# Four more first-weight loads inside the recurrence loop, and four reorderings in the last part of an mLSTM + soft-MoE kernel

## The chip, the cores and the metric

The kernel runs on one core of a Trainium2 chip. The metric is the device time of one execution in microseconds; three executions of the kernel before gave 192.66, 192.68 and 195.63 us, with a median of 192.68. One more execution was taken with the hardware profiler, and its trace is the source of all durations below.

## What is computed

Two parts follow each other. The first is a recurrent cell over 768 steps for 4 x 8 heads of width 40; its output is scaled by a sigmoid gate and becomes a matrix x of 3072 tokens x 320 features. The second is a soft mixture of experts: every token gets 32 logits, the 32 slots are weighted sums of all tokens, 8 experts each turn 4 slots through two layers, and every token takes a weighted sum of the slots' outputs.

```
for t in range(S):
    m_new = maximum(f[t] + m, i[t])
    C = exp(f[t] + m - m_new) * C + exp(i[t] - m_new) * outer(v[t], k[t])
    n = exp(f[t] + m - m_new) * n + exp(i[t] - m_new) * k[t]
    y[t] = sigmoid(o[t]) * (C @ q[t]) / maximum(abs(n . q[t]), 1)
x = y as (B * S, H * D)                 # 3072 x 320
logits = x @ phi                        # 3072 x 32
d = softmax of logits over the tokens   # per slot
slot_in = d.T @ x                       # 8 experts x 4 slots x 320
h = maximum(slot_in[e] @ w1[e], 0)      # w1: 8 x 320 x 1024
slot_out[e] = h @ w2[e]                 # w2: 8 x 1024 x 320
c = softmax of logits over the slots    # per token
out = c @ slot_out
```

## The kernel before, in words

The recurrence is computed in chunks. 24 steps (`NSTEP`) each handle 64 time steps of two of the four batches, so a step yields 128 tokens. Its products within the chunk are `scores` (queries times keys, into `psc`), the decay weights `ew` come from an exponential (`expo`), `mix_s` on VectorE (DVE) multiplies scores and weights, `mix_q` on GpSimd (POOL) multiplies the queries with their weights, in two instructions for the two batches, `keys` on VectorE scales the keys (`kr`), `state` carries the state on and `pv` forms the output in PSUM (`php`, later `phe` and `pzpsc`). `post_a_ops` and `post_b` divide and gate it into x, and `xtr` transposes x for the logits.

The order of all work is written out by hand; every engine runs its own instructions in program order. The main loop runs i from 0 to 20: iteration i loads KV for step i + 2, first weights (`load_w1`, 512 KB each) where i is in the list `W1L`, second weights (`load_wave`, 640 KB each, called waves) where `WVN` says so, the output gates of a group of four steps (`load_sig`, when i is a multiple of 4), and queries and keys for step i + 4; then it computes parts of steps i - 1 to i + 2. All these loads are issued by SyncE (SP) on one hardware queue, in program order. A load into a buffer that is still read makes SP wait, and all loads behind it.

Four steps are a group for the mixture of experts. For each group the loop forms the logits (`moe_pl`), the running maximum and the exponentials (`moe_nm_ops`, `ex_dT`), copies the logits (`ex_lt`, tile `lt`), transposes both and adds to the slots' running sum `acc` (`moe_psl`, `moe_acc`); `moe_e0`, `moe_e`, `comb_s` make the tokens' combine weights E, in two parts of reduced precision, and `comb_T`/`comb_h` transpose them and copy them to `cT`.

The last part begins after the loop. There step 21 is finished, steps 22 and 23 are done, and SP issues what is left of the 20 first weights and of the 16 waves; the waves reuse the buffers of the recurrence. Groups 4 and 5 (`gl - 1` and `gl`) are handled by hand: logits `pl4`, the product `psl4` in the same PSUM buffer, the final rescaling `a`, the slot inputs `psa` and `psb`, copied to `slT` by VectorE. `asum` is the slots' sum of exponentials, `pden` (one matmul with the selector `cden`) brings it to the slots' order, and `rd` is its reciprocal. `up` multiplies with the first weights in two halves of 512 columns (`phh`, `pzhm`), `relu` scales and clips, `turn` transposes, `down` multiplies with the waves, first for output columns 0 to 191 (`hf` = 0, `pso0`), then for 192 to 319. `gather` copies the result, `combine` forms the output blocks, and SP stores them. In the output loop over `PLAN` pieces of `down(1, ...)` stand between the output blocks.

Of the kernel before, what the change touches and what calls it, by code (L numbers as in the profile page):

```python
# [7 lines left out]
F32 = mybir.dt.float32  # L8
F32R = mybir.dt.float32r
# [9 lines left out]
DM = H * D  # L19
# [39 lines left out]
WV1 = 5  # L59
W1L = (2, 3, 5, 6, 7, 9, 10, 11, 14, 16, 18, 19, 20)  # L60

# [7 lines left out]
def kernel(ctx: ExitStack, tc: tile.TileContext, qk, kv, og, g0, g1, g2, consts, cinit, w1, w2, out):  # L69
# [230 lines left out]

    def mix_q(i):
        if i < 2 or i >= NSTEP:
            return
        t, w = KQ[i % NQ], ew[i]
        for a, r in enumerate(rows):
            nc.gpsimd.tensor_tensor(w[r, a], t[r, 1], w[r, a], ALU.mult)  # L306

# [119 lines left out]
    def ex_lt(gi, pl):  # L427
        run["lt"] = sb.tile([P, P], F32, tag="lt", name=f"lt{gi}")
        nc.scalar.copy(run["lt"], pl)
# [44 lines left out]

    def comb_T(tag=None, bufs=1, pc=None):
        e = run["E"]
        if pc is None:
            pc = pp.tile([P, GRP, P], F32, tag=tag, name="pc", bufs=bufs)
        for j in range(GRP):
            o = pc[:, 2 * (j % 2):2 * (j % 2) + 2, 64 * (j // 2):64 * (j // 2) + 64]  # L480
            nc.tensor.transpose(o.bitcast(F32R), e[:, 4 * j:4 * j + 4].rearrange("p g w x -> p (g w x)"), identr)
        return pc
# [17 lines left out]

    def comb_hi(e):
        E = run["E"] = sb.tile([P, GRP * NS // 8, 4, 8], F32R, tag="e", name="E")
        nc.scalar.copy(E[:, :, 0:2], bcast(e))

# [3 lines left out]

    def comb_s(gi, e):
        emit(comb_s_ops(gi, e))  # L510
        comb_n(e)
        comb_hi(e)
        comb_lo(e)
# [119 lines left out]
    post_b(i - 1)  # L633
    mix_q(NL)
    mix_s(NL)
    pv(i)
    scores(NL + 1)
# [41 lines left out]
    ex_dT(gl - 1)  # L679
    al4 = run["al"]  # L680
    moe_dT(gl - 1)
    pq = pp.tile([P, 2, 512], F32, tag="pe", name="pq")
# [11 lines left out]
    pd2 = [pq[:, 1, n * P:(n + 1) * P] for n in range(2)]  # L694
    ex_lt(gl - 1, pl4)
    moe_dT(gl, d=d5)
    load_wave()

    cden = d5_[:, 3 * P:]
    for t in slT + hT + [cden]:  # L700
        nc.gpsimd.memset(t, 0.0)
# [34 lines left out]
    for n, w in enumerate((128, 128, 64)):  # L736
        o = psa if n == 0 else psb[0:w, n - 1, :]
        nc.tensor.matmul(o, acc[:, n * P:n * P + w], selw, start=True, stop=True)
    pav = psa.rearrange("p (j r q) -> p j r q", j=4, r=2)
    pbv = psb.rearrange("p c (j r q) -> p c j r q", j=4, r=2)  # L740
# [8 lines left out]

    asum = sb.tile([P, 1], F32, tag="den", name="asum", bufs=ND)  # L750
    nc.vector.tensor_tensor(asum, a, acc[:, DM:DM + 1], ALU.mult)
    phh = [pp.tile([P, 512], F32, tag="ph", name="phh0"), pz[1]]
# [24 lines left out]
    CO = (0, HC0)  # L777
    pso = [pp.tile([P, HC[0]], F32, tag="pst", name="pso0"), pp.tile([P, 2, 512], F32, tag="pe", name="pso1")[:, 0, 0:HC[1]]]

# [47 lines left out]
    up(0, range(1, 2))  # L827
    pden = pp.tile([P, 1], F32, tag="pm", name="pden", bufs=2)
    nc.tensor.matmul(pden, cden, asum, start=True, stop=True)
    rd = sb.tile([P, 1], F32, tag="rl", name="rd", bufs=3)  # L830
# [4 lines left out]
    up(0, range(3, 5))  # L835
    comb_h(gl - 1, comb_T(pc=pz[0].rearrange("p (j t) -> p j t", j=GRP)))
    moe_e(gl, e0)
    h0 = relu(0)
    comb_s(gl, run["e"])
    up(1, range(1))  # L840
# [12 lines left out]
    for q, n in enumerate(PLAN):  # L853
        for h, x in rest[:n]:
            down(1, h, [x])
        rest = rest[n:]
        if q == 0:
            comb_h(gl, comb_T(pc=pz[0].rearrange("p (j t) -> p j t", j=GRP)))
        combine(0, QO[q])
    for h, x in rest:  # L860
# [79 lines left out]
```

## Time and profile before

| | |
|---|---|
| median of three executions | 192.68 us |
| the profiled execution's own time | 191.7 us |
| its span in the trace | 189.9 us |
| PE (TensorE) busy | 153.7 us, 81% of the span |
| DVE busy | 137.1 us, 72% |
| ACT (ScalarE) busy | 104.2 us, 55% |
| POOL busy | 105.3 us, 55% |
| DMA | 46.11 MB, mean 243 GB/s, 82.9% of 16 engines on the data queue |

In rows of the trace, times are in microseconds from the start of the span. PE is the matmul, PEld the weight load that overlaps it. "out<-in" are the program's names for tiles, x8 is a count, and the bracket at a row's end tells how long the engine was idle before it and what released it; "issue" there means that the profile shows nothing that it waited for. L785 is line 785 of the kernel before. Busy shares average over stages with different limits: the loop lasts until about 134 us, the last part until the end.

### The profile page before, as it was taken

To read this page: it belongs to the slowest core of one execution; us is meant where nothing else is said; L and a number is where in the kernel's file an instruction comes from. 1 tells how busy PE (TensorE), PEld (TensorE's weight loads), DVE (VectorE), ACT (ScalarE), POOL (GpSimd) and SP (SyncE) were. 2 spreads that over 40 slices of the span, in tenths; PEclk is the share of its full clock that TensorE was granted. 3 is DMA by queue.
4 is the path that set the end of the run, shared out by engine and by line. 5 is a ranking of instruction groups with operands and counts; after the bars stand their busy time and mean duration, and the time that the engine had idled before them with its cause. 6 is when DMAs were issued, how large, how long until landed. Compare 5 with 4: busy or idle time off the path is not lost.

```text
span 189.9 us, 7226 instructions
## 1 busy us (share of the span) xinstructions
PE 153.7 (81%) x3017; PEld 118.5 (62%) x3017; DVE 137.1 (72%) x302; ACT 104.2 (55%) x233; POOL 105.3 (55%) x120
## 2 busy tenths in 40 slices
PE   7639869886899777995979968799879899949940
PEld 2328757775688755884857857588767433618740
DVE  6896999799689957599987984689866465304440
ACT  5885507856288674684848757586824512004340
POOL 8970519995688993575865789347991511000000
PEclk9975979998799997899999999999999999999996
DMA  5999693749949499273997999959999999972996
GB/s 142 238 264 249 195 303 80 236 93 309 278 105 268 118 318 272 70 254 66 279 278 199 277 298 262 257 146 274 258 385 398 364 364 363 363 253 65 298 277 198
DMA packets 25424, 46.11 MB, mean 243 GB/s; under 512 B 2224, under 2 KB 16944, under 8 KB 25392
## 3 DMA queue, kind: packets, MB, share of 16 engines
q1 hardware_dynamic: 25392, 45.65, 82.9%
q8 instruction: 24, 0.39, 0.9%
q14 instruction: 8, 0.07, 0.1%
HBM read 41.71 MB, written 3.93 MB: 240 GB/s over the span
## 4 chain that ended last, share of the span: by engine, by line
PE 44%; DVE 17%; DMA 11%; issue 10%; POOL 6%; ACT 6%; SPq 2%; DVEq 0%; POOLq 0%; ACTq 0%
DMA w<-in_w_dram 8%; PE psc L299 7%; PE php L342 5%; POOL ew L306 4%; PE pst L332 4%; DVE ew L312 4%; PE pe L282 3%; PE php L343 3%; PE pt L380 3%; PE po L814 3%; PE pso L785 2%; PE phh L757 2%; PE pl L389 2%; DVE RR L259 2%; PE pst L331 2%
## 5 line engine op out<-in xcount | busy, mean ns | idle before, releaser
L306 POOL TENSOR_TENSOR ew<-KQ,ew 40x512 f32<-40x512 f32 (+1 forms) x44 | 63.7, 1447 | 3.4
L299 PE MATMUL psc<-KQ 40*64 40x64 f32 (+1 forms) x768 | 29.6, 228 | 7.9 <-issue 4.5
L365 POOL TENSOR_TENSOR x<-sig,den 128x320 f32<-128x320 f32 x21 | 15.7, 750 | 36.2 <-DVE den L357 32.1
L312 DVE TENSOR_TENSOR ew<-psc,ew 64x512 f32<-64x512 f32 x48 | 32.2, 671 | 1.6 <-PE psc L299 0.7
L299 PEld LDWEIGHTS psc<-KQ 40*64 40x64 f32 (+1 forms) x768 | 26.1, 141 | 10.4 <-issue 4.9
L342 PE MATMUL php<-KV,ew 104*64 104x41 f32 x352 | 26.0, 236 | 3.7 <-DVE rsum L491 1.9
L343 PE MATMUL php<-KV,ew 128*64 128x41 f32 x352 | 26.3, 237 | 2.4 <-issue 1.8
L342 PEld LDWEIGHTS php<-KV,ew 104*64 104x64 f32 x352 | 23.7, 144 | 6.3 <-issue 5.3
L316 DVE TENSOR_TENSOR kr<-KV,rl 128x640 f32<-128x640 f32 x22 | 26.9, 1221 | 0.6
L284 ACT ACTIVATE ew<-pe 128x1024 f32<-128x1024 f32 x24 | 24.5, 1020 | 4.3 <-PE pe L282 4.1
L332 PE MATMUL pst<-KV,kr 128*64 128x41 f32 x352 | 26.5, 238 | 0.0
L343 PEld LDWEIGHTS php<-KV,ew 128*64 128x64 f32 x352 | 23.6, 142 | 2.6 <-issue 1.9
L384 ACT COPY xT<-pt 128x384 f32<-128x384 f32 x23 | 10.9, 479 | 24.4 <-PE pt L380 24.3
L332 PEld LDWEIGHTS pst<-KV,kr 128*64 128x64 f32 x352 | 23.7, 145 | 0.2 <-issue 0.2
L331 PEld LDWEIGHTS pst<-KV,kr 104*40 104x40 f32 x352 | 18.0, 122 | 8.8 <-issue 5.3
L282 PE MATMUL pe<-RR,LL 128*128 128x512 f32 x48 | 18.5, 468 | 3.9 <-DVE LL L268 2.5
L331 PE MATMUL pst<-KV,kr 104*40 104x41 f32 x352 | 20.8, 215 | 0.0
L334 ACT COPY KV<-pst 40x328 f32<-40x328 f32 (+1 forms) x44 | 18.8, 426 | 1.8 <-PE pst L332 0.8
L259 DVE TENSOR_TENSOR RR<-Y,hmp 32x512 fp32r<-32x512 f32 x24 | 16.3, 679 | 0.9
L380 PE MATMUL pt<-cst,x 128*128 128x128 f32 x63 | 12.1, 303 | 0.9 <-POOL x L365 0.8
L266 ACT ACTIVATE LL<-Y,cst 32x64 fp32r<-32x64 f32 x38 | 11.1, 337 | 1.8 <-DVE Y L232 1.4
L282 PEld LDWEIGHTS pe<-RR,LL 128*128 128x128 f32 x48 | 7.9, 207 | 4.6 <-ACT KV L195 2.6
(199 smaller groups left out, 244.8 us busy)
## 6 DMA issues: line engine op xcount, KB each, us to landing
w<-in_w_dram SPq DMA_DIRECT2D x20, 512.0 KB, 7.2
w<-in_w_dram SPq DMA_DIRECT2D x15, 640.0 KB, 10.4
KV<-in_kv_dram SPq DMA_DIRECT2D x48, 162.0 KB, 5.6
KQ<-in_qk_dram SPq DMA_DIRECT2D x24, 320.0 KB, 6.3
sig<-in_og_dram SPq DMA_DIRECT2D x6, 640.0 KB, 5.3
out_dram<-ob SPq DMA_DIRECT2D x5, 384.0 KB, 3.3
out_dram<-ob SPq DMA_DIRECT2D x2, 512.0 KB, 5.0
w<-in_w_dram SPq DMA_DIRECT2D x2, 320.0 KB, 9.5
```

The lines of the kernel that those rows point to most:

```text
L259: a = lambda: nc.vector.tensor_tensor(RR[n][g0:g0 + 32], y[g0:g0 + 32].unsqueeze(1).broadcast_to([32, H, L]), hmp[g0:g0 + 32, 0:H].unsquee ...
L282: nc.tensor.matmul(pe[:, a], LL[:, n, a, :], RR[n], start=True, stop=True)
L284: nc.scalar.activation(ew[i], pe, AF.Exp)
L299: nc.tensor.matmul(psc[64 * a:64 * a + 64, h], t[r, 0, h], t[r, 1, h], start=True, stop=True)
L306: nc.gpsimd.tensor_tensor(w[r, a], t[r, 1], w[r, a], ALU.mult)
L312: nc.vector.tensor_tensor(w[r, a], psc[r], w[r, a], ALU.mult)
L316: e.tensor_tensor(kr[i % 2][:, :, :, R0:], KV[i % NK][:, :, 0:DM].rearrange("p a (h d) -> p a h d", h=H), rl[i].unsqueeze(3).broadcast_to( ...
L331: nc.tensor.matmul(pst[64:64 + D, h], k[0:104, 0, h, R0:], vc[0:104, 0, h], start=True, stop=True)
L332: nc.tensor.matmul(pst[0:64, h], k[:, 1, h], vc[:, 1, h], start=True, stop=True)
L334: nc.scalar.copy(nvc[r, a], pst[r])
L342: nc.tensor.matmul(ph[0:64, h, 0:V1], w[0:104, 0, h], vc[0:104, 0, h], start=True, stop=True)
L343: nc.tensor.matmul(ph[64:128, h, 0:V1], w[:, 1, h], vc[:, 1, h], start=True, stop=True)
```

## The change

- `W1L` gains iterations 4, 8, 12 and 17: 17 of the 20 first weights are loaded in the loop, 3 behind it. At 4, 8 and 12 the added load stands between the KV loads and `load_sig`, at 17 between the KV loads and a wave.
- Of step 22's two `mix_q` instructions the second goes from POOL to VectorE, behind `mix_s` of that step.
- `ex_lt(gl - 1)`, ScalarE's copy of group 4's logits, is emitted before `moe_dT(gl - 1)` and no longer after group 5's exponentials.
- `asum` is formed on ScalarE (a copy with a per-partition scale), and the matmul `pden` goes ahead of the up-projection, into a free part of the buffer `pq`. The selector's memset goes ahead of the other memsets; its copy stays behind them.
- Group 4's `comb_T`/`comb_h` move from the middle of the up-projection into the output loop, ahead of its second block. For this group 5's E gets a buffer of its own (tag RR1) and the transposes a free PSUM bank.

```diff
-W1L = (2, 3, 5, 6, 7, 9, 10, 11, 14, 16, 18, 19, 20)
+W1L = (2, 3, 4, 5, 6, 7, 8, 9, 10, 11, 12, 14, 16, 17, 18, 19, 20)
...
-    def mix_q(i):
+    def mix_q(i, batches=(0, 1), e=nc.gpsimd):
...
-        for a, r in enumerate(rows):
-            nc.gpsimd.tensor_tensor(w[r, a], t[r, 1], w[r, a], ALU.mult)
+        for a in batches:
+            r = rows[a]
+            e.tensor_tensor(w[r, a], t[r, 1], w[r, a], ALU.mult)
...
-    mix_q(NL)
+    mix_q(NL, (0,))
     mix_s(NL)
+    mix_q(NL, (1,), nc.vector)
     pv(i)
...
     al4 = run["al"]
+    ex_lt(gl - 1, pl4)
     moe_dT(gl - 1)
...
-    ex_lt(gl - 1, pl4)
     moe_dT(gl, d=d5)
     load_wave()
...
-    for t in slT + hT + [cden]:
+    for t in [cden] + slT + hT:
         nc.gpsimd.memset(t, 0.0)
...
         nc.tensor.matmul(o, acc[:, n * P:n * P + w], selw, start=True, stop=True)
+    asum = sb.tile([P, 1], F32, tag="den", name="asum", bufs=ND)
+    nc.scalar.activation(asum, acc[:, DM:DM + 1], AF.Copy, scale=a)
+    pden = pq[:, 1, 2 * P:2 * P + 1]
+    nc.tensor.matmul(pden, cden, asum, start=True, stop=True)
...
-    asum = sb.tile([P, 1], F32, tag="den", name="asum", bufs=ND)
-    nc.vector.tensor_tensor(asum, a, acc[:, DM:DM + 1], ALU.mult)
...
-    pden = pp.tile([P, 1], F32, tag="pm", name="pden", bufs=2)
-    nc.tensor.matmul(pden, cden, asum, start=True, stop=True)
...
-    comb_h(gl - 1, comb_T(pc=pz[0].rearrange("p (j t) -> p j t", j=GRP)))
+    E4 = run["E"]
     moe_e(gl, e0)
     h0 = relu(0)
-    comb_s(gl, run["e"])
+    comb_s(gl, run["e"], "RR1")
...
             comb_h(gl, comb_T(pc=pz[0].rearrange("p (j t) -> p j t", j=GRP)))
+        if q == 1:
+            comb_h(gl - 1, comb_T(pc=pso_[:, 1].rearrange("p (j t) -> p j t", j=GRP), e=E4))
         combine(0, QO[q])
```

More of the change, by code (lines that the diff above doesn't have):

```diff
@@ L472, in moe_comb2, with comb_T @@
         comb_h(gi, comb_T("pm", 2))
-    def comb_T(tag=None, bufs=1, pc=None):
-        e = run["E"]
+    def comb_T(tag=None, bufs=1, pc=None, e=None):
+        e = e or run["E"]
         if pc is None:
@@ L499, in comb_n, with comb_hi @@
         v.tensor_tensor(e, e, run["rsum"].unsqueeze(2).broadcast_to([P, GRP, NS]), ALU.mult)
-    def comb_hi(e):
-        E = run["E"] = sb.tile([P, GRP * NS // 8, 4, 8], F32R, tag="e", name="E")
+    def comb_hi(e, tag="e"):
+        E = run["E"] = sb.tile([P, GRP * NS // 8, 4, 8], F32R, tag=tag, name="E")
         nc.scalar.copy(E[:, :, 0:2], bcast(e))
@@ L507, in comb_lo, with comb_s @@
         v.tensor_tensor(E[:, :, 2:4], bcast(e), E[:, :, 0:2], ALU.subtract)
-    def comb_s(gi, e):
+    def comb_s(gi, e, tag="e"):
         emit(comb_s_ops(gi, e))
         comb_n(e)
-        comb_hi(e)
+        comb_hi(e, tag)
         comb_lo(e)
@@ L777 @@
     CO = (0, HC0)
-    pso = [pp.tile([P, HC[0]], F32, tag="pst", name="pso0"), pp.tile([P, 2, 512], F32, tag="pe", name="pso1")[:, 0, 0:HC[1]]]
+    pso = [pp.tile([P, HC[0]], F32, tag="pst", name="pso0")]
+    pso_ = pp.tile([P, 2, 512], F32, tag="pe", name="pso1")
+    pso.append(pso_[:, 0, 0:HC[1]])
     def down(hf, n, rk):
```

## The prediction

> **What bounds the kernel now.** I read the page first (its span below), then the chain that ended last, and then the part of the PE timeline to which that chain points.
>
> ```profile
> span 189.9 us, 7226 instructions
> ```
>
> ```profile
> 160.66 10.37 DMA w<-in_w_dram
> ```
>
> This piece of the chain is the last second-weight load (a wave). It is issued at 160.66, and the matmuls that use it start when it has landed, at 171.07. The PE timeline shows how long PE stood still for it and its forerunners:
>
> ```profile
> 163.97 2.16 PE L785 MATMUL pso<-w,hTa 128*32 128x192 f32 x48
> 165.94 0.83 PE L785 MATMUL pso<-w,hT 128*32 128x192 f32 x16
> 166.59 0.51 PE L785 MATMUL pso<-w,hTa 128*32 128x192 f32 x8
> 167.62 0.53 PE L785 MATMUL pso<-w,hTa 128*32 128x192 f32 x8 [0.52 <-DMA w<-in_w_dram]
> 169.50 0.53 PE L785 MATMUL pso<-w,hT 128*32 128x192 f32 x8 [1.34 <-DMA w<-in_w_dram]
> 171.07 0.53 PE L785 MATMUL pso<-w,hT 128*32 128x192 f32 x8 [1.03 <-DMA w<-in_w_dram]
> 171.42 0.84 PE L785 MATMUL pso<-w,hTa 128*32 128x128 f32 x24
> ```
>
> Unhindered, 48 matmuls go from 163.97 to 165.94, 0.041 us each. The 96 of the first output half that follow 163.97 would be through at 163.97 + 96 x 0.041 = 167.9; the next half starts at 171.42. **The stall is 3.5 us**: three idle times, and three times the refilling of PE. Why the loads are late is seen in the DMA view from 134 to 172 us (slices of 0.95 us) and in a table by stage (PE, PEld, DVE, ACT, POOL busy, PE clock, DMA share, GB/s):
>
> ```profile
> GB/s 254 286 230 334 345 410 375 397 418 414 414 418 387 345 368 358 364 362 362 364 363 373 358 365 362 365 362 364 362 360 362 365 369 354 369 358 302 152 35 0
> ...
> w<-in_w_dram SPq DMA_DIRECT2D x7, 512.0 KB, 7.6
> ```
>
> ```profile
> 38.50:41.20 2.70, 2.10 (x55) 1.84 (x52) 2.62 (x6) 2.33 (x6) 2.55 (x4) 1.00 0.29 68
> 61.70:64.00 2.30, 1.90 (x58) 1.69 (x53) 2.22 (x9) 1.16 (x4) 2.02 (x4) 1.00 0.31 84
> 86.20:88.80 2.60, 1.11 (x34) 1.04 (x32) 2.50 (x9) 0.51 (x2) 0.81 (x1) 1.00 0.14 31
> 113.60:124.20 10.60, 8.99 (x193) 7.00 (x193) 5.59 (x12) 7.12 (x18) 6.88 (x7) 1.00 1.06 265
> 124.20:127.60 3.40, 3.40 (x88) 2.92 (x85) 3.40 (x9) 2.96 (x7) 1.05 (x1) 1.00 0.43 105
> 174.80:188.40 13.60, 7.84 (x120) 6.63 (x118) 5.43 (x12) 4.49 (x11) 0.00 (x0) 0.92 0.97 290
> ```
>
> From 134 us to the last landing the DMA engines never rest: seven first weights go first, at some 410 GB/s, then the waves at some 364. The end part is bound by bytes, while the loop leaves holes (shares of 0.29, 0.31 and 0.14).
>
> **The change part by part.**
>
> *Four first weights more in the loop.* The end part loses 4 x 524,288 bytes, at 410 GB/s 5.1 us, and every wave lands that much earlier, the last near 166.0. What is late next is PE itself: with the other edits (-0.9 together ahead of this point, below) it comes to the last wave's matmuls at 171.07 - 3.5 - 0.9 = 166.7. So the whole stall goes, **-3.5**, with 0.7 us of cover; each us by which the end part's loads start later than that comes back one for one. Bounds: -3.0 with half a us lost so, -3.7 if a matmul is 0.039.
>
> *What they cost the loop.* Iterations 4, 8 and 12 issue the added load behind the KV loads and ahead of the sig load, for which SP waits anyway:
>
> ```profile
> SPq L140 <- POOL x L365: 14.1, 4, 4.4
> ```
>
> Four waits, 14.1 us together, up to 4.4: there lie the three holes, 2.70, 2.30 and 2.60 us long. One load at the loop's 265 GB/s takes 2.0 us and fits into each, and the sig and KQ issues behind it wait for nothing new. Iteration 17 has no hole (1.06 from 113.60 to 124.20), so 2.0 us of backlog pass on, to the KQ and wave issues behind it and the next KV loads; the stretch that follows, at 0.43, has 1.9 us idle and takes them up. The new tiles reuse buffers of the gates, all done before the new iteration. What a full DMA does hold up in the loop is PE's own instructions:
>
> ```profile
> 111.73:117.64 5.91, 5.42 (x125) 4.75 (x125) 3.74 (x8) 3.97 (x10) 5.68 (x5) 1.00 1.04 292
> 117.64:141.73 24.09, 21.22 (x503) 17.88 (x503) 19.05 (x41) 14.95 (x33) 16.62 (x15) 1.00 0.93 261
> ```
>
> ```profile
> 111.73 0.25 PE L343 MATMUL php<-KV,ew 128*64 128x41 f32 x1 [1.78 <-issue]
> ```
>
> ```profile
> 117.65 0.45 PE L299 MATMUL psc<-KQ 64*64 64x64 f32 x8 [0.49 <-issue]
> ```
>
> ```profile
> 141.73 0.20 PE L343 MATMUL phe<-KV,ew 128*64 128x41 f32 x1 [0.80 <-issue]
> ```
>
> ```profile
> q8 instruction: 24, 0.39, 0.9%
> ```
>
> Before these three rows PE stands with nothing to wait for. Between the first two lie 125 + 125 matmuls and weight loads, between the last two 503 + 503, four times as many; the 24 instruction packets (0.39 MB) serve them in blocks of about that size. I read it as PE coming to the end of a block before the next one is there, where the DMA share is 0.93 or more. Behind iteration 17 a block comes due at about 129, in a stretch that the backlog now fills. I take a little under the small stall of 0.49, **+0.3**; bounds 0 and 2.0 (a stall like the largest, 1.78, and something at iteration 8).
>
> [...]
>
> *One scaling of queries on VectorE.*
>
> ```profile
> 137.20 5.42 POOL L306 TENSOR_TENSOR ew<-KQ,ew 40x512 f32<-40x512 f32 x4
> 142.59 0.72 POOL L507 TENSOR_TENSOR E<-e,E 128x256 fp32r<-128x256 f32 x1
> ```
>
> ```profile
> 142.94 0.72 DVE L365 TENSOR_TENSOR xy<-sig,den 128x320 f32<-128x320 f32 x1
> ```
>
> ```profile
> L306 POOL TENSOR_TENSOR ew<-KQ,ew x44: 1256/1272/1942, 21.7 to 141.2; 40x512 f32<-40x512 f32 x22, 64x512 f32<-64x512 f32 x22
> ```
>
> ```profile
> L316 DVE TENSOR_TENSOR kr<-KV,rl x22: 817/1214/1639, 10.9 to 134.0; 128x640 f32<-128x640 f32 x22
> ```
>
> POOL loses one of four (5.42 / 4 = 1.36 us). The piece on VectorE is bounded by kr, 640 columns and both operands in the same memory: 0.82 at the least, 1.64 at the most; POOL's own stretch from 1.26 to 1.94. So I let the new piece queue behind POOL's first and end near 139.1, and hold POOL's next back by half a us. Behind it on VectorE stand the denominators, the sig product and the scores' scaling of the last steps, which PE waits for. POOL is done near 141.6 instead of 142.6, but PE doesn't go on before 141.73, when its instructions arrive, so the 1.36 isn't gained in full. What is gained is that L507 on POOL is over before the row of 142.94 starts: while the two overlap that row takes 0.72, and I let it fall by half. **-0.35**, bounds -1.3 (PE follows POOL) and +0.5 (the slip passes on).
>
> *Logits copied sooner.*
>
> ```profile
> 147.63 0.27 PE L689 MATMUL prow<-cst,nm 128*1 128x128 f32 x1
> 148.33 0.75 PE L442 MATMUL psl<-x,d 128*32 128x321 f32 x8 [0.44 <-ACT lt L429]
> ```
>
> ```profile
> 148.03 0.25 ACT L429 COPY lt<-pl 128x128 f32<-128x128 f32 x1
> ```
>
> psl is written where the logits stood and waits for this copy. Moved ahead of the copy of the transposed weights on ACT it is done long before; psl then starts behind prow, near 147.85: **-0.5**, bounds -0.44 (the idle time) and -0.6.
>
> *Slot sums on ScalarE, their product ahead.*
>
> ```profile
> 151.58 1.92 PE L757 MATMUL phh<-w,slTx 128*32 128x512 f32 x16
> 153.44 0.38 PE L829 MATMUL pden<-asum,d 128*128 128x1 f32 x2
> ```
>
> ```profile
> 151.63 0.20 POOL L701 MEMSET d<- 128x128 f32 x1
> 151.90 0.21 POOL L702 COPY d<-cst 128x32 f32<-128x32 f32 x1
> ```
>
> The product costs PE the same as before, only ahead of the up-projection. But it needs the selector that POOL copies at 151.90, behind all its memsets. The selector's own memset, 0.20, goes to an idle time, so the copy ends near 151.9 (on the old clock), while PE is free at 151.58: PE waits 0.3 to 0.4, and the whole up-projection stands behind it. **+0.4**, bounds 0 and +0.7 (product and wait). The sum itself, on ACT, is shorter than the 0.25 of the logits' copy or near it; behind it stand only a combine copy and an exponential that nothing on PE needs then.
>
> *The fourth group's combine transposes moved into the output loop.* Four transposes leave the stretch ahead of the wait and return before the second output block, with their copy on ACT. Once the stall is gone both places count alike for PE. The stores behind them fill 0.97 of the DMA's time (174.80:188.40), so the end follows the first store. **0**; bounds -0.5 (the stores close their gaps) and +0.6 (the first store late by the extra copy).
>
> *One more instruction block* comes due on PE near 168 while waves have just landed: **+0.1**, bounds 0 and 0.5.
>
> **Sum:** -3.5 + 0.3 - 0.35 - 0.5 + 0.4 + 0 + 0.1 = -3.55. (Ahead of the last wave: -0.5 - 0.35 + 0.4 and the moved transposes, -0.5, make the -0.9 above.) The profiled execution took 191.7 us, 1.8 beside its span: 191.7 - 3.55 = 188.15. The median shown, 192.68, lies 0.98 above it, and on that I forecast **189.1**.
>
> **The rivals.**
>
> *PE follows POOL.* The idle 0.80 before 141.73 falls away because other loads are in flight, the end part starts that much sooner, and the loop costs nothing: 189.1 - 0.8 - 0.3 = 188.0. For it: the idle times differ (1.78, 0.49, 0.80). Against: the DMA is as full there as before.
>
> *New waits in the new bound.* PE is now the bound, and what hits it counts in full: the selector wait at 0.7, the ACT copy at 0.6, the slip on VectorE at half its bound: 189.1 + 0.3 + 0.6 + 0.6 = 190.6. For it: each lies on PE's way. Against: each has some cover.
>
> *The change doesn't do what it says: SP, not bytes, paces the waves.*
>
> ```profile
> 134.51 4.12 SPq L147 DMA_DIRECT2D w<-in_w_dram x7
> ```
>
> Then four issues less bring the waves forward by 4 x 4.12 / 7 = 2.4 alone, PE's early 0.9 is lost in the wait that is left, and the moved transposes cost their 0.5 behind it: 192.68 - 2.4 + 0.5 + 0.3 = 191.1. Against: the GB/s stand flat at 364, as of a full DMA.
>
> *Instruction blocks late throughout the loop (slower).* Each added load pushes one block past its need, at the price of the row at 111.73, 1.78. Two of them, 3.6, are less than the gain without the loop's term (3.85); from the third on the kernel is slower: 192.68 - 3.85 + 3 x 1.78 = 194.2. For it: the stalls seen lie where the DMA is full. Against: a hole is filled with one load, not overfilled.
>
> **How the numbers follow.** Forecast 0.50, PE follows POOL 0.22, new waits 0.16, SP paces 0.07, late blocks 0.05. The range takes in 188.0 and part of the good bounds beyond it (-0.7 more), and on the poor side 191.1 with a large loop stall in part (+1.1): 187.3 to 192.2. A measurement of this kernel can tell about 2%, which is 188.8 on the good side. Beyond it lie most of the first rival (0.20) and four tenths of the forecast (0.20): faster 0.40. Over 196.5 it comes only with a fourth late block and more: 0.02. Within: 0.58.
>
> **What would show it.** Right: no DMA idle before pso in the first half and the last wave landing near 166; psl behind prow without a wait for lt; a PE gap before pden that POOL ends; the first store some 3.5 us earlier. Wrong: "w<-in_w_dram" still ahead of pso; more "issue" idle on PE between 36 and 130 us; the last KV loads issued later than before; a first store less than 3 us earlier.

## The result, and the profile after

The changed kernel takes **190.88 us** (median of 20 executions, 188.97 to 196.75) beside 194.13 us for the kernel before (20 executions, 191.16 to 202.92). The ratio is **0.9895, 95% interval 0.9861 to 0.9928**: about 1% faster, where the forecast was 3.55 us, 1.8% of the median shown. Single executions spread over 8 us (changed) and 12 us (before), with longer times at a lower granted clock (188.97 us at 0.954, 196.75 at 0.895), and the ratio is formed from the undisturbed ones alone. By the means of these 20 and 20 the gain is 3.54 us; in a later round, with 6 executions of the changed kernel and 23 of the kernel before, it is nil (194.06 and 194.03). Over all the executions measured in rounds the mean is 194.30 us for the kernel before (89 executions, standard error 0.27) and 192.05 us for the changed one (26, 0.51), 2.25 us less. So there is a gain, but its size is known to about a us only. That 190.88 lies inside the forecast's range says little, since in this measurement the kernel before gave 194.13 and not 192.68.

The profiled execution took 190.58 us, span 188.5. The first thing to read is where the loop ends, which is the last K/V issue on SP (the first row of its pair), and where the first store goes out. Before, then after (start, length, queue, line):

```profile
133.35 0.47 SPq L133 DMA_DIRECT2D KV<-in_kv_dram  x1
...
173.83 11.42 SPq L819 DMA_DIRECT2D out_dram<-ob  x11
```

```profile
136.04 0.47 SPq L133 DMA_DIRECT2D KV<-in_kv_dram  x1
...
172.25 11.74 SPq L825 DMA_DIRECT2D out_dram<-ob  x11
```

The loop ends 2.69 us later, the first store leaves only 1.58 us earlier. Counted from that K/V issue to the end of the span, the last part went from 56.57 to 52.45 us: -4.12, where the sum (without the loop's +0.3) had -3.85. So the last part did what was forecast, and the loop gave most of it back in these two executions. The last part first, on PE. The first output half of the kernel before starts here, and its waits are shown in the prediction:

```profile
161.97 1.48 PE L785 MATMUL pso<-w,hTa 128*32 128x192 f32 x32
```

The changed kernel:

```profile
163.22 1.48 PE L791 MATMUL pso<-w,hTa 128*32 128x192 f32 x32
...
165.22 2.16 PE L791 MATMUL pso<-w,hTa 128*32 128x192 f32 x48
167.19 0.83 PE L791 MATMUL pso<-w,hT 128*32 128x192 f32 x16
167.84 0.83 PE L791 MATMUL pso<-w,hTa 128*32 128x192 f32 x16
168.49 0.95 PE L791 MATMUL pso<-w,hT 128*32 128x192 f32 x16
169.26 0.84 PE L791 MATMUL pso<-w,hTa 128*32 128x128 f32 x24
```

No row of the first output half (128x192) waits for a wave any more, where before three did. From its first matmul to the first of the second half (128x128) it is 169.26 - 163.22 = 6.04 us, before 171.42 - 161.97, some 9.44. The last wave lands at 168.87, while its matmuls are already due: the cover of 0.7 us is not there. The holes in the loop are filled, as the windows show for the same stretches as before (DMA share and GB/s last):

```profile
38.50:41.20 2.70, 2.10 (x58) 1.85 (x53) 2.62 (x6) 2.39 (x6) 2.55 (x4) 1.00 0.76 237
61.70:64.00 2.30, 1.83 (x52) 1.62 (x52) 2.20 (x9) 1.15 (x5) 2.02 (x4) 1.00 0.99 210
86.20:88.80 2.60, 1.13 (x32) 1.04 (x32) 2.49 (x10) 0.82 (x2) 1.12 (x2) 1.00 0.64 153
113.60:124.20 10.60, 7.38 (x139) 5.82 (x141) 5.04 (x10) 5.06 (x15) 5.54 (x6) 0.76 1.06 271
```

The fourth row tells what went wrong: 139 matmuls where there were 193, at a granted clock of 0.76 instead of 1.00. The K/V issues of the iterations up to 18 come within 1.4 us of where they did; that of iteration 19 comes at 124.85 before and 127.54 after. PE's own row and the clock by slices (before, then after) show what lies there:

```profile
117.98 1.14 PE L299 MATMUL psc<-KQ 64*64 64x64 f32 x30 [2.16 <-issue]
```

```profile
PEclk9975979998799997899999999999999999999996
```

```profile
PEclk9995887999699999999999999669999999999995
```

A late instruction block held PE for 2.16 us, and from 119.11 to 125.94 its clock was halved (0.50 there; the two sixes in slices 26 and 27). Before, the same block was 0.49 us late, and 3.41 us of halved clock (0.50) lay at 73.62.

That such waits are late blocks is the author's reading, in the prediction from three rows; the trace's instruction packets agree with it. The packet ahead of this wait lies at 114.95 to 116.30, and PE goes on 1.68 us later. In the fifteen profiled executions 75 waits of PE after 27 us are marked "issue" and longer than 0.4 us, and every one ends 1.2 to 1.7 us after the end of an instruction packet. One more "issue" wait per execution, of 2.1 to 3.0 us at 25.5 to 26.2 us, is of another kind: no packet ends at that distance ahead of it, and it ends 0.1 us after VectorE's last product that reads the tile `psc`, which PE writes next.

### The profile page after: what moved, and what is told of

It is laid out like the page before. It is cut to its first block, busy times and chain, and to the rows that moved or that the text cites. A ratio compares the mean times of both kernels' runs of the same rounds, so it can differ in the third digit from the quotient of the medians.

```text
span 188.5 us, 7226 instructions
## 1 busy us (share of the span) xinstructions
PE 154.7 (82%) x3017; PEld 119.6 (63%) x3017; DVE 138.5 (73%) x302; ACT 104.7 (56%) x234; POOL 104.7 (56%) x119
## 4 chain that ended last, share of the span: by engine, by line
PE 58%; DVE 18%; issue 10%; POOL 5%; DMA 3%; ACT 3%; SPq 1%; DVEq 0%; ACTq 0%; POOLq 0%
PE psc L299 9%; PE php L343 5%; PE pso L791 5%; PE pst L333 5%; PE pe L282 4%; PE pt L381 4%; DVE ew L313 3%; PE php L344 3%; PE pl L390 3%; PE pw L156 3%; DVE kr L317 3%; DMA w<-in_w_dram 3%; PE po L820 2%; PE phh L761 2%; PE pzhm L761 2%
## 5 line engine op out<-in xcount | busy, mean ns | idle before, releaser
L307 POOL TENSOR_TENSOR ew<-KQ,ew 40x512 f32<-40x512 f32 (+1 forms) x43 | 62.9, 1463 | 3.2
L366 POOL TENSOR_TENSOR x<-sig,den 128x320 f32<-128x320 f32 x21 | 15.7, 750 | 38.3 <-DVE den L358 31.7
L299 PEld LDWEIGHTS psc<-KQ 40*64 40x64 f32 (+1 forms) x768 | 25.8, 140 | 11.8 <-issue 6.0
L343 PE MATMUL php<-KV,ew 104*64 104x41 f32 x352 | 25.6, 234 | 4.6 <-DVE rsum L492 1.8
L333 PE MATMUL pst<-KV,kr 128*64 128x41 f32 x352 | 27.4, 242 | 1.1 <-issue 1.1
L317 DVE TENSOR_TENSOR kr<-KV,rl 128x640 f32<-128x640 f32 x22 | 26.4, 1202 | 0.6
L344 PE MATMUL php<-KV,ew 128*64 128x41 f32 x352 | 26.2, 236 | 0.6 <-POOL ew L307 0.6
L333 PEld LDWEIGHTS pst<-KV,kr 128*64 128x64 f32 x352 | 24.6, 149 | 1.3 <-issue 1.3
L332 PEld LDWEIGHTS pst<-KV,kr 104*40 104x40 f32 x352 | 18.5, 124 | 8.9 <-issue 6.0
L332 PE MATMUL pst<-KV,kr 104*40 104x41 f32 x352 | 21.3, 217 | 0.0
L357 DVE SCALAR_TENSOR_TENSOR sig<-sig,php 128x320 f32<-128x320 f32 x22 | 10.5, 477 | 0.2
```

What stands on the lines that cost most here:

```text
L299: nc.tensor.matmul(psc[64 * a:64 * a + 64, h], t[r, 0, h], t[r, 1, h], start=True, stop=True)
L307: e.tensor_tensor(w[r, a], t[r, 1], w[r, a], ALU.mult)
L317: e.tensor_tensor(kr[i % 2][:, :, :, R0:], KV[i % NK][:, :, 0:DM].rearrange("p a (h d) -> p a h d", h=H), rl[i].unsqueeze(3).broadcast_to( ...
L332: nc.tensor.matmul(pst[64:64 + D, h], k[0:104, 0, h, R0:], vc[0:104, 0, h], start=True, stop=True)
L333: nc.tensor.matmul(pst[0:64, h], k[:, 1, h], vc[:, 1, h], start=True, stop=True)
L343: nc.tensor.matmul(ph[0:64, h, 0:V1], w[0:104, 0, h], vc[0:104, 0, h], start=True, stop=True)
```

## The experiments

Two questions were open. The first: does the loop's loss come from the added load of iteration 17 (theory A), from the four loads together through a fuller DMA and later instruction blocks, or from something that differs between executions whatever the loads are? The second: what is the freed stall in the last part worth? The expectations name their theories by letters and say what each stands for. "Halved" is time at half clock in the loop: the stretches that begin after 18 us and before the loop's end.

**Without the load of iteration 17 (no17).**

```diff
-W1L = (2, 3, 4, 5, 6, 7, 8, 9, 10, 11, 12, 14, 16, 17, 18, 19, 20)
+W1L = (2, 3, 4, 5, 6, 7, 8, 9, 10, 11, 12, 14, 16, 18, 19, 20)
```

> The changed kernel with 16 instead of 17 first weights in the loop, iteration 17's taken back into the last part. Theory A (iteration 17's load fills a stretch in which the DMA has no room, an instruction block reaches PE late, PE stands idle for about 2 us and its clock is halved for 6.8 us): the loop ends as early as before the change (last KV issue near 133.4 us, no idle of 2 us on PE about 118), the last part gives back about 1.2 us of the stall since every wave lands 1.3 us later; together 0.5 to 1 us faster than the changed kernel, ratio to the kernel before 0.984 to 0.987. Theory B (the halved clock falls on single executions by chance, and no load in the loop costs anything): only the 1.2 us are given back, ratio 0.995 to 0.997.

Measured: median 190.59 us (187.57 to 193.5), ratio 0.988 [0.969, 1.0069], too wide an interval to tell the theories apart. Its loop ended at 137.15, not earlier but 1.1 us later than with the load; PE again stood 1.34 us before the same matmul, and half clock came at 128.34. The wave stall grew, as one more load in the last part must make it:

```profile
169.84 0.53 PE L791 MATMUL pso<-w,hT 128*32 128x192 f32 x8 [0.60 <-DMA w<-in_w_dram]
171.42 0.53 PE L791 MATMUL pso<-w,hT 128*32 128x192 f32 x8 [1.04 <-DMA w<-in_w_dram]
171.77 0.84 PE L791 MATMUL pso<-w,hTa 128*32 128x128 f32 x24
```

**The same load two iterations later (late19).** One line: 17 leaves W1L and 19 issues two.

```diff
-            if i in W1L:
+            for _ in range(W1L.count(i)):
                 load_w1(len(w1_sb))
```

> The changed kernel with iteration 17's load moved to iteration 19, which then has two. Theory A: the stretch from 113 to 124 us is as before the change and the backlog falls into one with room; the loop loses 0.3 at most and the last part keeps all its gain, ratio 0.979 to 0.983. Theory B: the same as the changed kernel, 0.988 to 0.991.

Measured: median 192.11 us (190.53 to 196.93), ratio 1.0052 [0.9973, 1.0131], which neither theory had; by the means of all executions of these rounds it is 192.89 beside 193.97. In its profile the loop ended at 140.29 with 27.3 us of halved clock; from the K/V issue of iteration 17 to that of 19 it is 17.90 us without a load at 17, in no17 15.74, in the changed kernel 16.41. PE stood 2.51 us for a late block at 121.00 although no load had been added there. And in four kernels that do load at 17 (endfix, selfirst, after_pad, loads_alone, below) the same stretch takes 12.16 to 13.00 us, as in the kernel before (12.41, and 12.98 the second time). Theory A falls.

**The loads alone (loads_alone), the end's edits alone (end_alone).** The changed kernel with every edit of the last part undone, and the changed kernel with the old list of thirteen:

```diff
-W1L = (2, 3, 4, 5, 6, 7, 8, 9, 10, 11, 12, 14, 16, 17, 18, 19, 20)
+W1L = (2, 3, 5, 6, 7, 9, 10, 11, 14, 16, 18, 19, 20)
```

> The kernel before with the list of 17 first-weight loads alone, none of the other edits. Theory A: the stall of 3.5 us goes and the loop loses about 2, ratio 0.991 to 0.994. Theory B: the stall goes and the loop loses 0.3 at most, ratio 0.982 to 0.985.

> The changed kernel with the old list of 13 loads, so only the edits of the last part. Under both theories the waves land as late as before, PE's early 0.9 us is lost in the wait for them, and the combine transposes now stand behind the wait: 0.5 to 0.8 us slower than before, ratio 1.002 to 1.004. A rival, that the edits of the last part carry most of the gain, says 0.991 to 0.995.

Measured: loads_alone 192.98 us (187.59 to 197.24), by the means 1.4 us under the kernel before of these rounds (192.54 and 193.97); end_alone 197.04 us (193.56 to 202.27), ratio 1.0236 [0.9992, 1.0481], by the means 3.8 us slower where 0.5 to 0.8 was expected (six executions, and the interval reaches 1, so the size is open). In loads_alone the output half took 5.93 us and waited for no wave: the loads alone take the stall away. PE came late there (31.62 us after the loop's end, before 28.62), but by the rule further below it would not have waited on time either: the wave lets the second half start at 33.53, PE at 34.54. In end_alone it took 11.57, since PE came earlier to waves that came no sooner:

```profile
173.94 0.53 PE L791 MATMUL pso<-w,hTa 128*32 128x192 f32 x8 [0.87 <-DMA w<-in_w_dram]
175.77 0.87 PE L791 MATMUL pso<-w,hTa 128*32 128x192 f32 x8 [1.30 <-DMA w<-in_w_dram]
177.62 0.87 PE L791 MATMUL pso<-w,hT 128*32 128x192 f32 x8 [0.98 <-DMA w<-in_w_dram]
179.20 0.87 PE L791 MATMUL pso<-w,hT 128*32 128x192 f32 x8 [0.71 <-DMA w<-in_w_dram]
```

And its loop, the unchanged one, ended at 141.06, later than any with seventeen loads, with 30.7 us of halved clock.

**No first weight in the loop (loop_none), and one in each of twenty iterations (loop_all20).**

```diff
+W1L = ()
```

```diff
+W1L = tuple(range(1, 21))
```

> The changed kernel with no first weight loaded in the loop; all 20 come in the last part. A look at the loop: when its last KV load is issued, where PE stands idle for instructions, when its clock is halved. Theory C (a full DMA makes PE's instruction blocks late, and those idle times, not the loads themselves, set how long the loop takes from one execution to the next): with 13 to 17 loads less the blocks come in time, the loop ends before 131 us, no idle of over 1.5 us without a cause between 60 and 130 us, and no halved clock there. Theory D (the loop's length varies for another reason, the DMA has no part in it): it ends between 133 and 141 us as in the other executions. The last part is some 17 x 1.28 = 22 us longer under both, at 1.28 us a load.

> The changed kernel with all 20 first weights in the loop, one in every iteration. Theory C: the loop ends later than in most executions with 17, 138 to 142 us, with at least two idle times over 1.5 us and a halved clock behind one of them; the last part is PE's, no shorter than 52.4 us. Theory D: the loop as before, 133 to 137.

Measured: 214.45 us and 208.01 us, single executions, beside 197.67 for one of the kernel before. loop_none's loop still ended at 136.59 (a loop under 131 was expected if the loads made it long: a miss), with 17.1 us of halved clock. loop_all20's ended at 147.39, with 27.3, beyond what either theory had expected. Its waits on PE before 147 us (total, times, longest):

```profile
PE psc L299 <- issue: 8.0, 5, 2.7
...
PE pst L332 <- issue: 2.4, 2, 1.9
PE psc L299 <- DMA KQ<-in_qk_dram: 2.3, 2, 1.5
PE php L344 <- issue: 1.8, 1, 1.8
PE pst L333 <- issue: 1.7, 1, 1.7
```

The first row counts the wait near 25.6 us too (2.7 us), which is no late block. Without it these are 11.2 us of late blocks in eight places, and the loop's own queries are late. The changed kernel has 5.4 us in four places, the kernel before 3.6 in three (their first rows below count that early wait as well, 2.3 and 2.7 us):

```profile
PE psc L299 <- issue: 5.7, 3, 2.3
...
PE pst L333 <- issue: 1.1, 1, 1.1
...
PE php L343 <- issue: 0.9, 1, 0.9
```

```profile
PE psc L299 <- issue: 4.5, 3, 2.7
...
PE php L343 <- issue: 1.8, 1, 1.8
```

**The query scaling back on GpSimd (mixq_back).**

```diff
-    mix_q(NL, (0,))
+    mix_q(NL)
     mix_s(NL)
-    mix_q(NL, (1,), nc.vector)
```

> The changed kernel with both scalings of step 22's queries on POOL again. From the last KV issue to the end, 52.45 us in the changed kernel: by the prediction's term 0.35 more, 52.8; by the first rival (PE follows POOL) 1.3 more, 53.7; by its poor bound 0.5 less, 51.9. If the clock is halved within the last part, the stretch up to the transposes of step 22 is compared alone.

Measured: 195.32 us, a single execution with a long loop (139.20). What tells is the distance from the loop's end to the transposes of `xy` (steps 21 and 22): 10.38 us before, 9.74 after, 10.38 here. GpSimd's row is back at four pieces of 1.36 us:

```profile
143.05 5.42 POOL L307 TENSOR_TENSOR ew<-KQ,ew 40x512 f32<-40x512 f32 x4
148.44 0.72 POOL L508 TENSOR_TENSOR E<-e,E 128x256 fp32r<-128x256 f32 x1
```

So in this execution the edit is worth 0.64 us. Without the edit the distance is 10.38 in before_pad too, whatever late blocks lie in the stretch (0.80 us before, 1.06 in before_pad, 0.25 here). With it, at the full clock, the distance is shorter where the blocks are less late: 8.71 in no17 and 9.26 in end_alone (0.45 and 0.37 us late), 9.74 in after and 9.97 in selfirst (0.90 and 1.01). So the edit gains 0.4 to 1.7 us, by how late PE's instructions are.

**The selector first, and the moved transposes later (endfix); the selector first alone (selfirst).**

```diff
-    for t in [cden] + slT + hT:
-        nc.gpsimd.memset(t, 0.0)
+    nc.gpsimd.memset(cden, 0.0)
     nc.gpsimd.tensor_copy(cden..., ccol(C_SEL, NS)...)
+    for t in slT + hT:
+        nc.gpsimd.memset(t, 0.0)
```

```diff
-        if q == 1:
+        if q == 3:
             comb_h(gl - 1, comb_T(...))
```

> The changed kernel with two repairs: the selector is copied right behind its own memset, ahead of the others, and group 4's combine transposes come ahead of the fourth output block in place of the second. By the trace of the changed kernel PE waited 0.25 us for the selector, the up-projection's start lies 0.6 us later than without the product ahead, and ScalarE's extra copy held the first store back by 0.5 us and PE by 0.2: the part from the last KV issue to the end shrinks from 52.45 to between 51.4 and 52.0. If the stores set the end alone, only the first store's 0.5 counts with what stands ahead of it, 51.7; if neither is on the way to the end, it stays at 52.4.

> The changed kernel with the copy of the selector put right behind its own memset on GpSimd, ahead of the seven other memsets. If the 0.64 us by which the up-projection started later was the wait of the denominator matmul for that copy, TensorE's gap ahead of that matmul (0.25 us) is gone and the distance from the first slot matmul to the first of the up-projection goes from 1.47 to about 1.15 us, what was measured with this edit beside another one; the last part is then 0.2 to 0.4 us shorter than the changed kernel's where no halved clock falls into it. In the rounds 0.3 us is less than these kernels vary by: ratio to the kernel before 0.98 to 0.995, not to be told from the changed kernel's. If the delay is the matmul itself and not the wait, the distance stays at 1.4 to 1.5 us.

Measured: endfix 192.29 us (one execution), selfirst 192.1 us (188.1 to 194.1), ratio 0.9826 [0.9761, 0.9891], which overlaps the changed kernel's interval. From the first slot matmul to the first of the up-projection it is 1.47 us after and 1.15 in both of these, as expected. PE after, then GpSimd after, then PE of selfirst:

```profile
152.42 0.38 PE L740 MATMUL psa<-d,acc 128*128 128x32 f32 x2
...
153.57 0.38 PE L744 MATMUL pq<-asum,d 128*128 128x1 f32 x2 [0.25 <-POOL d L704]
153.89 1.92 PE L761 MATMUL phh<-w,slTx 128*32 128x512 f32 x16
```

```profile
150.84 0.32 POOL L703 MEMSET slTx<- 128x256 f32 x1 [5.52 <-PE psl L443]
...
153.31 0.21 POOL L704 COPY d<-cst 128x32 f32<-128x32 f32 x1
```

```profile
151.59 0.38 PE L741 MATMUL psa<-d,acc 128*128 128x32 f32 x2
...
152.42 0.38 PE L745 MATMUL pq<-asum,d 128*128 128x1 f32 x2
152.74 1.50 PE L762 MATMUL phh<-w,slTx 128*32 128x512 f32 x12
```

The copy stood behind memsets that had themselves waited 5.52 us for a buffer that psl reads. In endfix the first store goes out 1.29 us behind the scaled half, as before, and not 1.86 as after; but from the start of the second output half to the end it is 19.32 us, no less than the changed kernel's 19.23 (before: 18.51). So the first store does not set that end; what does was not tested, though the chain that ended last runs there over PE's output projection and output blocks.

**Both kernels again (before_again, after_again).** No edit.

> The kernel before once more, against itself. Theory L (the loop's length is set anew in each execution by where the halved TensorE clock and the late instruction blocks fall, whatever the loads): the profiled loop ends somewhere between 133.4 and 141.1 us after the span's start, longer by about 0.33 us for each us of halved clock in it beyond the 10.2 us that the first profile of this kernel had, iterations 18 and 19 show a late block with TensorE idle for 1 to 3 us, and the time is 191 to 200 us; the last part is as before, 56.6 us from the last K/V issue to the end unless halved clock falls in it, with the stall of 9.4 us between the first matmul of the first output half and the first of the second. Theory A (the loop was 2.7 us shorter because iteration 17 had no first weight to load): the loop ends within 0.7 us of 133.35 again and iterations 18 and 19 are as short as they were. The ratio to the kernel before is 1 under both, and the width of its interval is what five rounds can tell.

> The changed kernel once more. Theory L: the loop ends between 134 and 140 us, by its own share of halved clock; from the last K/V issue to the end 52.5 us, plus 1 to 2 us if halved clock falls into it; the median over the rounds lies about 2 us (1 to 3.5) under that of the kernel before, ratio 0.982 to 0.995. Theory A: the loop ends at 136.0 again within 0.7 us, and the ratio is the same; the two differ in the profile alone, in whether iterations 18 and 19 cost the same 2.7 us.

Measured: before_again 194.05 us (191.6 to 197.99), ratio to itself 1.0022 [0.9972, 1.0073]; after_again 195.77 us from six executions (187.69 to 197.38), where a median about 2 us under the kernel before was expected: a miss, with a mean equal to the kernel before of the same rounds. The loops ended at 134.63 and 136.63, with 13.7 us of halved clock each: the kernel before came 1.28 us later than the first time, where theory L had 0.33 x 3.4 = 1.1 for its halved clock and theory A at most 0.7; the changed one fits both, but from the K/V issue of iteration 17 to that of 19 it took 14.35 us this time instead of 16.41.

What came of the gain is seen in the last part. In both profiles 6.83 us of halved clock fell into the last part, ahead of the output projection (window, PE busy ..., PE clock, DMA share, GB/s; before_again, then after_again):

```profile
143.50:150.40 6.90, 6.46 (x77) 5.20 (x81) 3.22 (x11) 1.97 (x6) 1.15 (x4) 0.51 1.04 388
```

```profile
147.10:154.00 6.90, 6.61 (x80) 5.17 (x83) 3.19 (x13) 1.80 (x6) 0.00 (x0) 0.51 1.07 364
```

What these 6.83 us make of the first output half, before_again, then after_again:

```profile
172.82 0.53 PE L785 MATMUL pso<-w,hT 128*32 128x192 f32 x8 [1.01 <-DMA w<-in_w_dram]
173.17 0.84 PE L785 MATMUL pso<-w,hTa 128*32 128x128 f32 x24
```

```profile
174.06 0.83 PE L791 MATMUL pso<-w,hT 128*32 128x192 f32 x16
174.71 0.84 PE L791 MATMUL pso<-w,hTa 128*32 128x128 f32 x24
```

Counted from the last K/V issue, PE came to the output projection 2.78 us later than in the first profile of the kernel before (31.40 for 28.62), and to the second half only 0.47 later (38.54 for 38.07): it had waited there anyhow. In the changed kernel PE came 4.98 later (32.16 for 27.18) and reached the second half 4.86 later (38.08 for 33.22). The last part took 57.14 us in the one and 57.34 in the other: **in this pair of executions the whole gain was gone**. The stall that the change removes was also the cushion for whatever makes PE late ahead of it. The halved clock is not all of that lateness: between the loop's end and the output projection after_again has 3.11 us of late instruction blocks (after 0.90), before_again none (before 0.80).

**A known delay in both kernels (before_pad, after_pad).** 28 more matmuls ahead of the second half of the up-projection; the output is the same.

```diff
+    for _ in range(7):
+        for j in range(4):
+            nc.tensor.matmul(phh[1][32 * j:32 * j + 32, :], slc[0][:, j, :], w1_sb[5 * j][:, 512:1024],
+                             start=True, stop=True, tile_position=(0, 32 * j))
     up(1, range(1))
```

> The kernel before, with 28 more matmuls of 32 x 512 ahead of the second half of the up-projection (its first input chunk computed seven times more, each overwritten; nothing of the output changes), which by the 0.42 us of such a group of four keep TensorE some 3 us longer ahead of the output projection at the full clock. Theory S (the stall on the last wave is a cushion): the first matmul of the output projection comes 3 us later than in the kernel before, the first of its second half less than 0.6 us later, the stall shrinks from 9.4 to about 6.5 us, and the time is that of the kernel before within 0.6 us: ratio 0.997 to 1.004. Theory L (both kernels pay for each delay of TensorE alike, and the forecast was off through the loop alone): the whole last part is 3 us longer, ratio 1.012 to 1.018.

> The same 28 matmuls in the changed kernel. Theory S: nothing covers them, the first matmul of the output projection and the first of its second half both come 3 us later, the stall stays at about 6.0 us, the last part grows by 2.7 to 3.2 us from 52.5, and the ratio to the kernel before goes from 0.983 to 0.99 up to 0.998 to 1.006: the same delay then costs 0 in the one kernel and 3 us in the other. Theory L: the same 3 us here too, so that the two padded kernels still differ by the 2 to 3 us by which the two kernels differ.

Measured: before_pad 198.58 us (195.42 to 199.53), ratio 1.0229 [1.0126, 1.0332]; after_pad 199.22 us (196.93 to 201.41), 1.0255 [1.0141, 1.0368]. The delay was mis-sized: each matmul has two records, a group of four takes 0.86 us and not 0.42, so it is 6.0 us, more than the cushion. By theory S that is 6.0 - 3.5 = 2.5 us for the kernel before and 6.0 for the changed one; by the means of all executions it was 3.9 and 7.2, 1.3 us more each than that, and 3.4 us apart (standard error some 1.2) where the cushion is 3.5. By theory L the two padded kernels should still have differed by 2 to 3 us in favour of the change; they are level. Neither waits for a wave, before_pad, then after_pad:

```profile
176.67 0.83 PE L785 MATMUL pso<-w,hT 128*32 128x192 f32 x16
177.32 0.84 PE L785 MATMUL pso<-w,hTa 128*32 128x128 f32 x24
```

```profile
175.72 0.83 PE L791 MATMUL pso<-w,hT 128*32 128x192 f32 x16
176.37 0.84 PE L791 MATMUL pso<-w,hTa 128*32 128x128 f32 x24
```

**One rule for all of them.** With P the first matmul of the output projection and D the landing of the last wave, both counted from the last K/V issue, the second half starts at the later of P + 5.92 (PE's own time for the first half, from after_again) and D + 0.39 (from the kernel before):

| kernel | P | D | the later of the two | second half starts | end |
|---|---|---|---|---|---|
| before | 28.62 | 37.67 | 38.06 (D) | 38.06 | 56.57 |
| before_again | 31.40 | 38.15 | 38.54 (D) | 38.54 | 57.14 |
| before_pad | 36.32 | 38.42 | 42.24 (P) | 42.24 | 60.58 |
| end_alone | 27.20 | 38.09 | 38.48 (D) | 38.78 | 59.11 |
| after | 27.18 | 32.83 | 33.22 (D) | 33.22 | 52.45 |
| no17 | 26.63 | 34.22 | 34.61 (D) | 34.62 | 53.74 |
| selfirst | 27.13 | 33.76 | 34.15 (D) | 34.15 | 53.55 |
| loads_alone | 31.62 | 33.14 | 37.54 (P) | 37.55 | 56.15 |
| late19 | 29.69 | 33.39 | 35.61 (P) | 35.62 | 54.62 |
| mixq_back | 29.14 | 32.86 | 35.06 (P) | 35.06 | 54.34 |
| endfix | 29.01 | 33.82 | 34.93 (P) | 34.93 | 54.25 |
| after_again | 32.16 | 33.66 | 38.08 (P) | 38.08 | 57.34 |
| after_pad | 35.98 | 35.14 | 41.90 (P) | 41.91 | 61.19 |

It holds to 0.02 us but for end_alone, where halved clock fell on the last matmuls themselves (0.87 us for a row of eight, at the full clock 0.53). With thirteen loads D decides, until PE is 3.5 us late. Beside the changed kernel's P of 27.18 that reserve is 0.1 to 1.1 us with seventeen loads and 1.5 with sixteen. In all six of those kernels with a P in the fourth column halved clock lay ahead of the output projection, and after_pad has its 28 matmuls too.

How late PE comes follows from two things. A straight line through the thirteen rows (6.01 us taken off for the pads) gives 0.53 us of P (standard error 0.05) for each us of halved clock between the loop's end and the output projection, 0.55 (0.12) for each us of late blocks there, and -1.3 (0.2) for the edits of the last part, with 0.4 us left over.

**The loop over thirteen executions.** With halved clock and the loop's end: before 10.2 and 133.35, before_again 13.7 and 134.63, before_pad 13.7 and 135.08, end_alone 30.7 and 141.06 (thirteen loads); after 13.7 and 136.04, after_again 13.7 and 136.63, selfirst 13.7 and 134.94, endfix 13.7 and 136.03, after_pad 10.2 and 134.46, no17 13.7 and 137.15, loads_alone 20.5 and 135.95, mixq_back 23.9 and 139.20, late19 27.3 and 140.29 (sixteen or seventeen). A straight line through them gives 0.33 us of loop (standard error 0.04) for each us of halved clock, and 0.83 us (0.55) for the added loads, with 0.9 us left over for a single execution. With the late blocks as a third term, 0.59 (0.14) for each us of them, it leaves 0.6 us, and nothing for the loads as such (-0.1, 0.5): the late blocks of the loop take 3.7 us on average with thirteen loads and 5.3 with sixteen or seventeen. So, as far as such a line can show it, the added loads lengthen the loop by way of PE's instructions, as the prediction argued.

## Why the prediction was wrong

The direction and the mechanism of the last part were right; the size was not. By the prediction's steps:

- **The stall, -3.5 with 0.7 us of cover.** The stall went (9.44 to 6.04 us, loads alone 5.93). The failed step is the sentence "What is late next is PE itself", priced as if PE always came at one time. Without the pads it comes between 26.6 and 32.2 us after the loop's end, by halved clock and late blocks. Before, up to 3.5 us of that cost nothing; after, all but a reserve of 0.1 to 1.1 costs in full. So the last part changed by -4.1, -3.0 (selfirst) or -2.8 (no17) where no halved clock lies ahead of the output projection, and +0.2 where 6.83 us do (after_again beside before_again). The cover was nil too: P + 5.92 is 33.10 in the changed kernel and D + 0.39 is 33.22, since PE came 1.44 us earlier and not 0.9, and D moved by 4.84 in this execution and by 3.9 in selfirst, where 5.1 was forecast. The expectation that the last wave lands near 166 missed by 2.9, 2.7 of it the later loop.
- **The loop, +0.3 (0 to 2.0).** The profiled loop was 2.69 us longer, outside the bounds. Over thirteen executions it is 0.83 (0.55), which agrees with the term and, by the late blocks, with its reason. What failed is the base: one execution stood for the loop, and it is the shortest of the thirteen, with the least halved clock (as after_pad). Nor was the load of iteration 17 the cause: without it the same stretch was as long, and with it in four other kernels as short as before. With twenty loads the loop ended some 8 us beyond the line above at its halved clock (130.5 + 0.33 x 27.3 = 139.5, measured 147.39), with 11.2 us of late blocks in it; that a full DMA brings these about was the author's reading and is not shown: from 113.60 to 124.20 its DMA share was 1.06, as in both kernels. Whether the late blocks bring the halved clock about is not shown.
- **The scaling on VectorE, -0.35 (-1.3 to +0.5).** -0.64 in the profiled execution, inside the bounds; in no17 and end_alone -1.67 and -1.12, by how late PE's instructions were. VectorE's piece took 1.71 us, a little over its upper bound of 1.64, but GpSimd's L508 was over sooner and the sig product that had taken 0.72 beside it takes 0.49, as argued:

```profile
139.99 1.71 DVE L307 TENSOR_TENSOR ew<-KQ,ew 64x512 f32<-64x512 f32 x1
...
145.62 0.49 DVE L366 TENSOR_TENSOR xy<-sig,den 128x320 f32<-128x320 f32 x1
```

- **Logits copied sooner, -0.5.** Right: psl follows prow without a wait, at 0.19 us instead of 0.70.

```profile
149.81 0.27 PE L692 MATMUL prow<-cst,nm 128*1 128x128 f32 x1
150.00 0.75 PE L443 MATMUL psl<-x,d 128*32 128x321 f32 x8
```

- **Slot sums and their product, +0.4 (0 to +0.7).** Right in place and size: the up-projection starts 0.64 us later behind the first slot matmul, 0.32 of it for the selector (selfirst), the rest the product, which came later on PE before; so 0.32 is the net price.
- **The moved transposes, 0 (-0.5 to +0.6).** About right, with a wrong reason. From the first matmul of the up-projection to the output projection PE takes 9.33 us instead of 10.38, of which 0.31 is the product's place, so some -0.7 there; from the start of the second output half to the end it is 19.2 us on average where it was 18.5, +0.7. "The end follows the first store" was the wrong reason: endfix brought the first store back and not the end.
- **One more instruction block, +0.1.** None was late near 168 us. The one at 144.39 (0.90 us) has its like before (0.80 at 141.73), but in other executions of the last part late blocks add up to 3.1 us ahead of the output projection, and with the stall gone they are no longer hidden there.

Of the rivals, "new waits in the new bound" (190.6) came nearest, and its premise, that what hits PE now counts in full, was what the runs showed; that its number came near is luck, since the delays it listed were others. "SP paces the waves" falls: D moved by 4.84 us in the changed kernel and 3.91 in selfirst, not 2.4. "Late blocks throughout" is too much for seventeen loads (5.4 us of them in the loop, before 3.6), while with twenty there are five more than before. "PE follows POOL" had the wrong premise, since PE still waits for its instructions there; but where they were less late, in no17 and end_alone, PE gained about all of the 1.36.

The terms do not add up to one exact number. By the rows above, the second half starts at 38.3 us on average in before and before_again and at 35.1 in the seven kernels with the changed last part and no pad that have sixteen or seventeen loads; with +0.7 behind it and +0.8 in the loop that is -1.7, beside -2.25 (0.6) measured over all executions and 1.05% by the ratio.

How much of the shortfall the lost cushion makes is not shown, since only the profiled executions tell where the halved clock fell (ahead of the output projection in eight of the thirteen). Over all executions in rounds whose clock is on record, 70 and 26, the time rises by 0.31 us for each us of halved clock in both kernels (standard errors 0.03 and 0.05); that the changed kernel pays more for it cannot be seen in so coarse a number, since most of the halved clock lies in the loop. The changed kernel also had less of it, 26.4 us on average where the kernel before had 30.2; at 0.31 that is 1.2 of the 2.25 us, and whether the change or luck brought it is open.

## What to carry to other kernels

A wait for a transfer can also be a cushion, of 3.5 us here: before its removal is priced, ask how late the engine may come to it for nothing, and how often it does, since after the removal each such delay beyond the reserve that is left (0.1 to 1.1 us here) counts in full. A sum made against one profiled execution inherits that execution's luck (two executions of the kernel before ended their loops 1.28 us apart); look at the clock row first, and where it differs from slice to slice take a second execution before a term of half a us is believed. A copy that a moved matmul needs must be moved past everything that waits on its engine's queue, not only given its memset early: here it stood behind memsets that had waited 5.52 us, and PE paid 0.32 us for it.

## What the runs showed of the hardware

The clock of PE was halved for part of the loop in every profiled execution, for 10.2 to 30.7 us of it. In the first profile of the kernel before the stretches that begin there after 18 us lasted 3.41 us each and began at 25.8, 46.3 and 73.6 us; in that of the changed kernel they lasted 3.41, 3.41 and 6.83 us and began at 27.0, 47.4 and 119.1, at a clock of 0.50 to 0.51 in all six. PE was busy for 3.43 of 3.43 us in the stretch at 73.6, for 5.77 of 6.83 at 119.1, and for 6.46 and 6.61 of 6.90 us in the two windows above; in the last 3.64 us of the span before, at 0.50 too, it had no matmul. By the straight lines above a us of it cost 0.33 us in the loop and 0.53 ahead of the output projection. Instruction blocks on PE are late with thirteen loads, and with none: 3 waits and 3.6 us in the loop of the kernel before, and in loop_none 2 waits and 3.6 us, beside the early wait of 2.1 us that this row counts too:

```profile
PE psc L299 <- issue: 5.7, 3, 2.1
```
